# The channel transform of a Fourier mix for half of the frequencies, its even and odd parts joined by VectorE

## The chip, the cores and the metric

One core of a Trainium2 chip. The metric is the device time of one execution in microseconds (us), as a median over several executions; the profile shows one execution, whose span is some 2 us shorter than its time. TensorE is the matrix engine, VectorE and ScalarE are the element-wise engines (DVE and ACT in the profile). PE in the profile is TensorE's products and PEld the loading of their weights, one of the two operands of a product. PSUM is the memory that TensorE writes its sums into. On one core an execution counts as slow when it takes over 1.5% more than the fastest of its kernel.

## The reference, cut to what matters

A block-sparse attention (cut) gives `x`, 4 batches of 768 rows and 512 channels, fp32. Then, for each batch:

```python
X = np.fft.fft(x, axis=1)          # along the 768 rows
X = np.fft.fft(X, axis=2)          # along the 512 channels
u = x + np.real(X)
un = (u - mean(u)) / sqrt(var(u) + 1e-6)      # over the channels
out = u + np.maximum(un @ w_ch1, 0.0) @ w_ch2   # 512 -> 2048 -> 512
```

## The kernel before

All products are fp32. In a batch the row transform leaves `yt` (in the profile: `big`), whose 512 channels are folded into four groups of 128: groups 0 and 1 serve the even output channels, groups 2 and 3 the odd ones. The channel transform then works through six tiles of 128 rows. A tile takes four products with 256 columns each, and one VectorE add puts the result onto `x`:

```python
fd = bpool.tile([P, 6, HD], FP, ...)              # P = 128, HD = 256, DM = 512
fetch(out=fd, in_=dr["fd"].ap())
# ...
for half in range(2):
    # ...
    for i in range(HT):                           # HT = 3: six tiles per batch
        t = HT * half + i
        ps = bank([P, 2, HD], f"mx_{b}_{t}")
        cols = slice(P * i, P * (i + 1))
        for par in range(2):                      # even, odd output channels
            nc.tensor.matmul(ps[:, par, :], yt[:, half, 2 * par, cols], fd[:, 3 * par, :],
                             start=True, stop=False)
            nc.tensor.matmul(ps[:, par, :], yt[:, half, 2 * par + 1, cols], fd[:, 3 * par + 1 + half, :],
                             start=False, stop=True)
        xv = x[:, t, :].rearrange("p (m two) -> p two m", two=2)
        tt(xv, ps, xv, ADD)                       # one add, 512 columns
        nc.vector.bn_stats(out=bst, in_=x[:, t, :])
        nc.vector.bn_aggr(out=stat[:, i], in_=bst)
        yield
    # ... a dozen short VectorE steps: 1/sqrt(var), shift (tile `norm`)
for t in range(NST):                              # six tiles again
    # un = x * scale + shift, on ScalarE and VectorE in turn
    for d in range(NDT):
        nc.tensor.transpose(ps[:, d // 2, d % 2, :], un[:, t, P * d:P * (d + 1)], ident)   # `unt`
    # copied to u[...] by ScalarE and VectorE in turn
    yield
_right_sums(tt, lambda i: u[:, i])                # then the hidden layer `hx` may start
```

A list scheduler decides in what order the engines get this. For batches 1 to 3 it places pieces of the transform between output products of the batch before, which are the filler (`ox`, `oy`, `oz`):

```python
drive((gen_fourier(b + 1), 22, 600), (last, 12, 0))
```

In batch 0 the companion of the transform is attention work instead.

## Time and profile before

| | before |
|---|---|
| time, median of 3 (lowest to highest) | 853.1 us (852.67 to 853.25) |
| profiled span | 852.3 us |
| TensorE busy, of it | 820.0 us, 96% |
| VectorE busy | 470.9 us, 55% |
| `mx` stage of batch 2 (six tiles on TensorE) | 10.36 us |
| first `mx` product to first hidden product `hx`, batches 1, 2, 3 | 48.10, 41.52, 41.71 us |

The last row is the distance on TensorE's timeline from the first product of the changed stage to the first product of the hidden layer. It contains everything that the change touches in a batch, and it does not contain the attention at the start, whose length differs by some microseconds from one execution to the next. The lines of the page and of the timelines that carry the argument are shown in the prediction below. One more, of TensorE's timeline of before in batch 1 (columns: start us, duration us, engine, line, operation, output and inputs, shape, count, and in brackets the idle time and its releaser), shows that the stage was not wholly without waits:

```profile
277.32 1.53 PE L1045 MATMUL unt<-ident,big 128*128 128x128 f32 x12 [0.45 <-ACT big L1038]
```

### The profile page before, as it was taken

What the parts mean: (1) busy time and instruction counts of PE and PEld (TensorE: products, weight loads), DVE (VectorE), ACT (ScalarE), POOL (GpSimd) and SP (SyncE); (2) the same over time, 40 slices, a digit from 0 to 9 for tenths busy, and PEclk for the clock granted to TensorE, in tenths of its full rate; (3) what the DMA queues carried; (4) which work ended last, traced back from release to release, by engine and by line L of the source; (5) the groups of instructions that cost most, each with busy time, mean ns of one, the idle gap of its engine ahead of it and who ended that gap; (6) DMA issues with size and microseconds to landing.
All of it is one profiled execution on the core that took longest, in us unless ns stands there. A gap on an engine that the chain in (4) does not pass through costs nothing.

```text
span 852.3 us, 14372 instructions
## 1 busy us (share of the span) xinstructions
PE 820.0 (96%) x5970; PEld 573.8 (67%) x5970; DVE 470.9 (55%) x1061; ACT 230.4 (27%) x473; POOL 36.9 (4%) x44
## 2 busy tenths in 40 slices
PE   6979998999999999999999999999999999999997
PEld 5847755545557455787667875688667885686586
DVE  2487996986966343544356933443337843432352
ACT  3524666542722013122231103120321102101100
POOL 3200011003000200001000000000000000000000
PEclk8989999999999999999999999999999999999999
DMA  9998695979523273454843136403412316205001
GB/s 217 230 273 161 163 228 175 277 247 303 187 97 120 74 270 129 121 111 156 238 123 105 69 115 229 106 28 81 170 61 75 112 51 258 87 1 215 1 25 53
DMA packets 102857, 122.31 MB, mean 143 GB/s; under 512 B 50592, under 2 KB 83584, under 8 KB 102784
## 3 DMA queue, kind: packets, MB, share of 16 engines
q1 hardware_dynamic: 102240, 121.14, 48.6%
q8 instruction: 49, 0.80, 0.4%
q10 hardware_dynamic: 544, 0.17, 0.1%
q14 instruction: 24, 0.20, 0.1%
HBM read 97.18 MB, written 24.12 MB: 142 GB/s over the span
## 4 chain that ended last, share of the span: by engine, by line
PE 80%; DVE 9%; ACT 6%; DMA 2%; issue 1%; POOL 1%; ACTq 0%; DVEq 0%; POOLq 0%
PE hx L1067 18%; PE ox L1133 14%; PE hz L1067 9%; PE o L1108 7%; PE oz L1133 7%; PE hy L1067 4%; PE y L984 4%; PE oy L1133 3%; PE mx L1005 2%; PE sc L727 2%; PE mx L1007 2%; ACT kt L670 2%; ACT qt L670 2%; DVE x L552 1%; PE sc L687 1%
## 5 line engine op out<-in xcount | busy, mean ns | idle before, releaser
L1067 PE MATMUL hx<-u,w 128*128 128x384 f32 x512 | 186.1, 492 | 8.0 <-ACT h L1077 6.0
L1067 PEld LDWEIGHTS hx<-u,w 128*128 128x128 f32 x512 | 94.4, 190 | 74.7 <-ACT h L1077 9.3
L1067 PE MATMUL hz<-u,w 128*128 128x384 f32 x256 | 93.2, 486 | 0.0
L1108 PE MATMUL o<-w,h 128*128 128x512 f32 x192 | 84.7, 595 | 0.0
L1067 PEld LDWEIGHTS hz<-u,w 128*128 128x128 f32 x256 | 48.6, 190 | 33.9 <-ACT h L1084 0.2
L1133 PE MATMUL ox<-w,s 128*128 128x256 f32 x288 | 69.0, 381 | 0.4 <-DVE x L552 0.3
L1133 PE MATMUL oz<-w,s 128*128 128x256 f32 x288 | 68.6, 380 | 0.0
L1133 PE MATMUL ox<-w,h 128*128 128x256 f32 x288 | 67.3, 380 | 0.0
L1108 PEld LDWEIGHTS o<-w,h 128*128 128x128 f32 x192 | 35.8, 190 | 42.4 <-issue 40.4
L552 DVE TENSOR_TENSOR x<-ox,x 128x256 f32<-128x256 f32 x72 | 30.4, 422 | 57.5 <-PE ox L1133 57.5
L1133 PEld LDWEIGHTS oz<-w,s 128*128 128x128 f32 x288 | 54.6, 190 | 8.1 <-DVE x L552 0.8
L1133 PEld LDWEIGHTS ox<-w,s 128*128 128x128 f32 x288 | 54.1, 190 | 8.5 <-DVE x L552 1.2
L1133 PEld LDWEIGHTS ox<-w,h 128*128 128x128 f32 x288 | 54.2, 190 | 8.2
L552 DVE TENSOR_TENSOR h<-hx,h 128x384 f32<-128x384 f32 x32 | 17.8, 556 | 71.6 <-PE hx L1067 71.6
L1077 ACT COPY h<-hx 128x384 f32<-128x384 f32 x32 | 15.3, 478 | 139.4 <-PE hx L1067 127.8
L552 DVE TENSOR_TENSOR h<-hy,h 128x384 f32<-128x384 f32 x32 | 17.8, 556 | 56.9 <-PE hy L1067 53.7
L1067 PE MATMUL hy<-u,w 128*128 128x384 f32 x128 | 46.5, 486 | 0.0
L984 PE MATMUL y<-fs,fold 128*128 128x193 f32 x192 | 37.3, 337 | 0.0
L1093 ACT ACTIVATE h<-hx 128x384 f32<-128x384 f32 x32 | 15.7, 490 | 79.0 <-PE hx L1067 79.0
L984 PEld LDWEIGHTS y<-fs,fold 128*128 128x128 f32 x192 | 31.5, 191 | 8.0 <-issue 6.3
L671 DVE TENSOR_REDUCE km<-kt 128x24 f32<-128x768 f32 x16 | 15.2, 951 | 37.8 <-ACT kt L670 25.2
L1067 PEld LDWEIGHTS hy<-u,w 128*128 128x128 f32 x128 | 24.3, 190 | 17.0
(120 smaller groups left out, 1103.3 us busy)
## 6 DMA issues: line engine op xcount, KB each, us to landing
w<-dw SPq DMA_DIRECT2D x40, 896.0 KB, 5.0
words<-in_moe_w_ch_dram SPq DMA_DIRECT2D x32, 512.0 KB, 6.5
vw<-in_v_dram SPq DMA_DIRECT2D x47, 192.0 KB, 6.3
dw<-w SPq DMA_DIRECT2D x8, 896.0 KB, 7.7
kn<-in_k_dram SPq DMA_DIRECT2D x16, 384.0 KB, 4.9
qn<-in_q_dram SPq DMA_DIRECT2D x16, 384.0 KB, 5.6
vb<-in_v_dram SPq DMA_DIRECT2D x32, 192.0 KB, 5.7
out_dram<-x SPq DMA_DIRECT2D x24, 256.0 KB, 2.1
```

The source lines that it names most:

```text
L552: nc.vector.tensor_tensor(out=out, in0=in0, in1=in1, op=op)
L670: nc.scalar.copy(out=dst[D * e:D * (e + 1), s:S:2], in_=ps[D * s:D * (s + 1)])
L671: nc.vector.tensor_reduce(out=km[:, 0:nb], in_=kt[:, W:W + S].rearrange("p (n f) -> p n f", f=BLOCK), op=ALU.max, axis=AX.X)
L727: nc.tensor.matmul(ps[h][r:r + 64, i, :], kt[rows, o:o + 64], qt[rows, o:o + BLOCK], start=True, stop=True)
L984: nc.tensor.matmul(y, fgs[par][:, st, P * g:P * (g + 1)], fs[par][:, g % 2, st, :], start=(st == 0), stop=(st == HT - 1))
L1005: nc.tensor.matmul(ps[:, par, :], yt[:, half, 2 * par, cols], fd[:, 3 * par, :], start=True, stop=False)
L1007: nc.tensor.matmul(ps[:, par, :], yt[:, half, 2 * par + 1, cols], fd[:, 3 * par + 1 + half, :], start=False, stop=True)
L1067: nc.tensor.matmul(ps, w[:, a, kk, :], u[:, r, kk, :], start=start and kk == 0, stop=stop and kk == 1, skip_group_check=True)
L1077: nc.scalar.copy(out=c11, in_=X)
L1093: nc.scalar.activation(out=c21, in_=X, func=AF.Relu)
L1108: nc.tensor.matmul(ps, h[:, n, hf, P * t:P * (t + 1)], wt[2, b, j][:, 2 * hf:2 * hf + 2, :], start=(n, hf) == (0, 0), stop=(n, hf) == (NC ...
L1133: nc.tensor.matmul(ps, left[a][:, n, :], wt[2, b, j][:, r, :], start=start and n == 0, stop=stop and n == NC - 1, skip_group_check=True)
```

## The change

The real part of the transform is symmetric but for a sign: if E is the even part of output channel c and O the odd part, channel c is E + O and channel 512 - c is E - O (signs turned in the second half of the rows). So E is needed for channels 0 to 256 and O for 1 to 255 only: 512 columns per tile in place of 4 x 256 = 1024. One input row that belongs to E was stored in the group that feeds O (row 0 of group 1); it gets a product of its own with a single row, which accumulates onto E. That is the fifth product. VectorE then makes four adds of what was one, two of them reading the columns backwards. The table shrinks from 1536 to 641 columns, and the change holds for batches 1 to 3; batch 0 keeps the old form. The diff, with blank lines and the change of the returned dictionary cut:

```diff
# table
+    fd = g["fd"].reshape(P, 6, DM // 2)
+    n = DM // 4
+    odd = fd[:, 1, 1:n].copy()
+    odd[0] = 0.0
+    fm = np.concatenate([fd[:, 0, 0:n + 1], fd[:, 3, 0:n], odd, fd[:, 4, 0:n], fd[:, 1, 0:n + 1]], axis=1)
# ... fetched as `fm` where b > 0, `fd` where b == 0
+    def mix_halves(ps, y, fm, xt, half):
+        Q = DM // 4
+        e0, e1, o0, o1, row = (fm[:, a:z] for a, z in ((0, Q + 1), (Q + 1, HD + 1), (HD + 1, HD + Q),
+                                                      (HD + Q, DM), (DM, DM + Q + 1)))
+        for out, g, table, last in ((ps[:, 0:HD + 1:2], 0, e0, False), (ps[:, 1:HD:2], 2, e1, True),
+                                    (ps[:, HD + 2:DM:2], 1, o0, True), (ps[:, HD + 1:DM:2], 3, o1, True)):
+            nc.tensor.matmul(out, y[:, g], table, start=True, stop=last, skip_group_check=True)
+            if not last:
+                nc.tensor.matmul(out, y[0:1, 1], row[0:1], start=False, stop=True, skip_group_check=True)
+        low, high = xt[:, 1:HD], xt[:, HD + 1:DM]
+        tt(xt[:, 0:HD + 1], ps[:, 0:HD + 1], xt[:, 0:HD + 1], ADD)
+        tt(high, ps[:, HD - 1:0:-1], high, ADD)
+        tt(low, low, ps[:, HD + 1:DM], SUB if half else ADD)
+        tt(high, high, ps[:, DM - 1:HD:-1], ADD if half else SUB)
# in the loop over the tiles
-                ps = bank([P, 2, HD], f"mx_{b}_{t}")
+                if b:
+                    mix_halves(bank([P, DM], f"mx_{b}_{t}"), yt[:, half, :, cols], fd, x[:, t, :], half)
+                else:
+                    ps = bank([P, 2, HD], f"mx_{b}_{t}")
-                for par in range(2):
+                for par in range(0 if b else 2):
-                xv = x[:, t, :].rearrange("p (m two) -> p two m", two=2)
-                tt(xv, ps, xv, ADD)
+                if b == 0:
+                    xv = x[:, t, :].rearrange("p (m two) -> p two m", two=2)
+                    tt(xv, ps, xv, ADD)
```

More of the change, by code (lines that the diff above doesn't have):

```diff
@@ L450, in _tables @@
     fs = np.ascontiguousarray(np.moveaxis(g["fs"], 2, 0))
+    fd = g["fd"].reshape(P, 6, DM // 2)
[3 more added lines that the diff above has]
+    fm = np.concatenate([fd[:, 0, 0:n + 1], fd[:, 3, 0:n], odd, fd[:, 4, 0:n], fd[:, 1, 0:n + 1]], axis=1)
+    fm = np.ascontiguousarray(fm)
     return dict(wide=wide, near=near, sel=sel.reshape(4 * nb, 2, P), half=half.reshape(P, 2), count=count, fs=fs,
-                fd=g["fd"], ident=g["ident"])
+                fd=g["fd"], fm=fm, ident=g["ident"])
 A11, A12, S3, A22, S1, S2_, S4 = range(7)
@@ L928, in get_tables @@
             fs.append(t)
-        fd = bpool.tile([P, 6, HD], FP, tag=tag, bufs=bufs, name=f"fd_{b}")
-        fetch(out=fd, in_=dr["fd"].ap())
+        if b:
+            fd = bpool.tile([P, C["fm"].shape[1]], FP, tag=tag, bufs=bufs, name=f"fm_{b}")
+            fetch(out=fd, in_=dr["fm"].ap())
+        else:
+            fd = bpool.tile([P, 6, HD], FP, tag=tag, bufs=bufs, name=f"fd_{b}")
+            fetch(out=fd, in_=dr["fd"].ap())
         tables[b] = fs, fd
@@ L1001, in gen_fourier @@
                 t = HT * half + i
-                ps = bank([P, 2, HD], f"mx_{b}_{t}")
                 cols = slice(P * i, P * (i + 1))
-                for par in range(2):
+                if b:
+                    mix_halves(bank([P, DM], f"mx_{b}_{t}"), yt[:, half, :, cols], fd, x[:, t, :], half)
+                else:
+                    ps = bank([P, 2, HD], f"mx_{b}_{t}")
+                for par in range(0 if b else 2):
                     nc.tensor.matmul(ps[:, par, :], yt[:, half, 2 * par, cols], fd[:, 3 * par, :],
```

## The prediction

> **What bounds the kernel now.** I read the page first: engine totals, the slices, the chain of waits. Then the tile view of `mx` (the accumulator of the channel transform) and the timeline of TensorE and VectorE around one of the changed stages.
>
> ```profile
> span 852.3 us, 14372 instructions
> PE 820.0 (96%) x5970; PEld 573.8 (67%) x5970; DVE 470.9 (55%) x1061; ACT 230.4 (27%) x473; POOL 36.9 (4%) x44
> PE   6979998999999999999999999999999999999997
> PE 80%; DVE 9%; ACT 6%; DMA 2%; issue 1%; POOL 1%; ACTq 0%; DVEq 0%; POOLq 0%
> ```
>
> TensorE is the bound: 96% busy, and in slices of 21 us it drops below nine tenths only near the start and in the last slice. So removed TensorE time is worth its full length if TensorE isn't made to wait instead.
>
> ```profile
> L1005 PE MATMUL mx<-fd,big x96: 379/379/483, 75.7 to 669.3; 128*128 128x256 f32 x96
> L1007 PE MATMUL mx<-fd,big x96: 378/379/379, 78.2 to 669.7; 128*128 128x256 f32 x96
> L552 DVE TENSOR_TENSOR x<-mx,x x24: 656/682/692, 82.3 to 670.4; 128x512 f32<-128x512 f32 x24
> ```
>
> 24 tiles (6 per batch), 192 records: every fp32 product leaves two records (two passes), so a tile is 4 products of 256 columns, 8 passes. The 379 ns is a latency, not a cost; cost is the step from start to start, and the timeline has it:
>
> ```profile
> 464.00 0.59 PE L1005 MATMUL mx<-fd,big 128*128 128x256 f32 x2
> 464.43 0.59 PE L1007 MATMUL mx<-fd,big 128*128 128x256 f32 x2
> ...
> 473.93 0.59 PE L1007 MATMUL mx<-fd,big 128*128 128x256 f32 x2
> 474.36 1.89 PE L1133 MATMUL ox<-w,s 128*128 128x256 f32 x8
> ...
> 478.81 1.52 PE L1045 MATMUL unt<-ident,big 128*128 128x128 f32 x12
> 480.16 1.89 PE L1133 MATMUL ox<-w,h 128*128 128x256 f32 x8
> ```
>
> Two passes of 256 columns take 0.43 us, 0.216 each; the stage of six tiles is 474.36 - 464.00 = 10.36 us without a gap. Twelve passes of 128 columns (the transposes `unt`) take 480.16 - 478.81 = 1.35 us; without their slow start 0.109 each. Time is thus proportional to columns, and halving the columns halves it. Between the two lie output products of the previous batch (`ox`, `oz`), the filler that hides VectorE's normalisation.
>
> ```profile
> 465.93 0.69 DVE L552 TENSOR_TENSOR x<-mx,x 128x512 f32<-128x512 f32 x1 [6.05 <-PE mx L1007]
> 466.65 0.69 DVE L1012 BATCH_NORM_STATS2 bst<-x 128x6 f32<-128x512 f32 x1
> 467.38 0.18 DVE L1013 BATCH_NORM_AGGREGATE stat<-bst 128x2 f32<-128x6 f32 x1
> 468.95 1.29 DVE L552 TENSOR_TENSOR x<-mx,x 128x512 f32<-128x512 f32 x2 [1.39 <-PE mx L1007]
> ```
>
> In this stage VectorE waits for TensorE (6.05 and 1.39 us). The sums of `u` end at 487.67 + 2.69 = 490.36, and the hidden layer, which needs them, starts only at 505.52:
>
> ```profile
> 487.67 2.69 DVE L552 TENSOR_TENSOR u<-u 128x768 f32<-128x768 f32 x3
> 490.27 0.42 DVE L552 TENSOR_TENSOR x<-oz,x 128x256 f32<-128x256 f32 x1
> 490.60 0.68 DVE L552 TENSOR_TENSOR s<-s,h 128x512 f32<-128x512 f32 x1
> ```
> ```profile
> 505.52 1.45 PE L1067 MATMUL hx<-u,w 128*128 128x384 f32 x4
> ```
>
> So some 15 us of slack stand behind the stage. (490.27 to 490.60 is VectorE's step for 256 columns: 0.33 us, for a record of 0.42.)
>
> **What the Trainium skill says.** "TensorEngine Tiling (Array Packing)", Key Properties: changing the tiling mode drains TensorE. The changed kernel does that: its product with one row runs in a 32-row mode. The trace of before has such switches, at the one-column products `zq`, and agrees:
>
> ```profile
> 454.11 0.49 PE L988 MATMUL y<-fs,zq 128*1 128x193 f32 x2
> 454.53 0.59 PE L984 MATMUL y<-fs,fold 128*128 128x193 f32 x2
> 455.05 0.82 PE L988 MATMUL y<-fs,zq 128*1 128x193 f32 x4
> 455.80 3.87 PE L984 MATMUL y<-fs,fold 128*128 128x193 f32 x22
> ```
>
> An undisturbed pass of 193 columns takes 0.163 us. From 454.11 to 454.53 two passes and a switch take 0.42: the drain is 0.09. From 454.53 to 455.05 two passes and a switch take 0.52: 0.10 more. That is the weight load, which can't run ahead across the switch. "TensorE: Matmul & The Clock Gate", LDWEIGHTS, says that a load's time goes with its columns, not its rows, 128 columns at 1.2 GHz = 107 ns; it fits the 0.10, and the one-column load shows none. The one-row product loads 128 columns, so it should pay 0.10 on the way in as well; no run shows that yet.
>
> "PSUM — Partial Sum Buffer", Specifications, says that a non-contiguous access pattern slows matmuls significantly; here two products per tile write every second word. The trace of before disagrees for this form:
>
> ```profile
> 30.02 1.48 PE L660 MATMUL qk<-ident,qn 128*64 128x128 f32 x24
> ```
>
> These also write every second column, two at a time in two halves of the array: (1.48 - 0.27)/23 = 0.053 per record, 0.106 per pass in each half, full rate. I book no cost. "VectorE: DVE Perf Modes", the TRN2 errata, has (N+151)/0.96 ns for an fp32 add: 424 for 256, and the record above is 0.42. It fits.
>
> **The change part by part**, for batches 1 to 3, 18 tiles; batch 0 is untouched.
>
> TensorE, columns. Removed per tile: 8 passes x 0.216 = 1.73 us. Added: five products (129, one-row 129, 128, 127, 128 columns), 10 passes x 0.109 = 1.09 us. Saved 0.64 per tile, 3.8 per batch, 11.5 in all.
>
> TensorE, switches. By the order of instructions the one-row products of tiles 1 and 2 stand side by side, the others alone: 5 round trips per batch. Each 2 x 0.09 + 2 x 0.10 = 0.39 us; 2.0 per batch, 5.9 in all. Net on TensorE 5.6 us. The stage should take 10.36 - 3.8 + 2.0 = 8.5 us.
>
> VectorE. One add of 512 (step 0.60) becomes four of 255 to 257, 3 x 0.335 + 0.42 = 1.43 until the statistics may start: +0.75 per tile, 4.5 per batch, 13.5 in all (470.9 becomes about 484). The reads run backwards and from PSUM; I take no extra for it. Most lies in the waits of 6.05 and 1.39 us and in the slack. What reaches TensorE is where it needs a result at a fixed place in its order. Walk through batch 2, from the start of the stage: tile 0 done at 1.9; four adds and statistics to 3.9; eight adds (2.8, from 4.1, when tile 1 is there) and two statistics to 8.2; twelve adds and the norm's dozen short steps (0.08 each beside them) to 13.2; the pending `ox` add 13.6; three statistics and the first normalised tiles at 16.2 and 16.7. TensorE: stage 8.5, with output products of 0.43 around it the next use of `ox` at 14.2 (ready, 13.6), and the transposes at 16.0. It waits about 0.5 us, in batches 2 and 3, 1.0 in all. In batch 1 the order puts 12 products of 0.86 us each, 10.4 us, before the transposes, which come at 18.9 while VectorE is ready near 16: no wait.
>
> DMA. The table shrinks from 1536 to 641 columns, three times; the view shows no wait of TensorE for it. Nothing.
>
> Sum: 853.1 - 11.5 + 5.9 + 1.0 = **848.5 us**.
>
> **The rivals.** First, VectorE becomes the bound of the stage: 18 tiles give back all their 0.75 us, +13.5 against -5.6, some 861. For it: TensorE works through six tiles in 8.5 us and VectorE needs about 13, and four banks serve both. Against it: 6.05 and 1.39 us of waiting to fill, filler that the new order places later (in batch 1, 6 us more of it before the transposes), 15 us of slack. Second, the switches are free or hidden: 848.5 - 5.9 = 842.6. Against it: every such switch in the trace of before shows its 0.09. If only the load into the one-row product is hidden, 15 x 0.10 less, 847. Third, strided writes do slow the products: two of five run at half rate, 18 x 2 x 0.22 = 8 us more, 856. Against it: the transposing products above at full rate. Fourth, the whole column saving shows nowhere because another chain sets the end: 853. Against it: TensorE without a gap from the stage to the hidden layer.
>
> **Range and chances.** The mildest mix (cheaper switches, no wait) gives about 845, a VectorE that waits 1 us more per batch 851.5. Range 845.0 to 851.5. Faster by 2% would need 17 us, more than the whole column saving of 11.5: 0.01. Slower by 2% would need the first rival at full force and more: 0.01. Within 2%: 0.98.
>
> **What would show it.** TensorE's records rise by 36, VectorE's by 54. `mx` passes of 128 columns stand 0.109 apart; each one-row product has 0.2 us extra before or in it, and as much after. The stage is 8.5 us, not 6.6 (switches free) or over 10 (strided writes slow, or waiting for banks). Transposes wait for the normalised tile by about half a microsecond in batches 2 and 3. Wrong if TensorE waits for VectorE's `x` or for a bank within the stage, or if the hidden layer starts right after the sums of `u`.

## The result, and the profile after

| | before | after |
|---|---|---|
| time, median of 4 (lowest to highest) | 853.13 us (852.67 to 853.25) | 848.13 us (847.39 to 849.99) |
| ratio, 95% interval | | 0.9946 (0.9928 to 0.9963) |
| `mx` stage of batch 2, filler inside it left out | 10.36 us | 8.63 us |
| first `mx` to first `hx`, batches 1, 2, 3 | 48.10, 41.52, 41.71 | 45.59, 39.83, 40.04 |
| their sum | 131.33 | 125.46 |

A ratio, here and below, is the mean time of one kernel's fast runs over that of the other's of the same rounds, so it is not quite the ratio of the medians. The change saves 5.0 us by the medians, half a per cent: within 2%, near the 848.5 us of the prediction. The three distances account for 5.87 us, which lies inside the interval of the ratio (0.0037 x 853 = 3.2 to 0.0072 x 853 = 6.1 us).

The span and the engine totals of the page after:

```profile
span 846.1 us, 14497 instructions
PE 813.9 (96%) x6006; PEld 569.1 (67%) x6006; DVE 479.4 (57%) x1115; ACT 230.5 (27%) x473; POOL 36.3 (4%) x44
```

TensorE has 36 records more (a product of one row is two records, and there are 18) and VectorE 54 (18 tiles with 3 adds more), both as foretold. TensorE is as full as before, 96%: the saving came off the bound. The tile view of `mx` after (count, then duration in ns as lowest/median/highest, first and last start, shapes) shows what a tile now consists of:

```profile
L963 PE MATMUL mx<-fm,big x144: 273/275/377, 258.2 to 664.4; 128*128 128x128 f32 x72, 128*128 128x129 f32 x36, 128*128 128x127 f32 x36
L965 PE MATMUL mx<-fm,big x36: 270/270/373, 258.5 to 663.5; 1*128 1x129 f32 x36
```

Do not read costs out of these durations. 270 ns is how long a pass stays in the pipe, and by it the one-row product looks no dearer than the others. The cost is in the steps between starts, on TensorE's timeline of after in batch 2:

```profile
461.10 0.39 PE L963 MATMUL mx<-fm,big 128*128 128x129 f32 x2
461.41 0.48 PE L965 MATMUL mx<-fm,big 1*128 1x129 f32 x2
461.83 1.38 PE L963 MATMUL mx<-fm,big 128*128 128x128 f32 x10
463.14 0.71 PE L965 MATMUL mx<-fm,big 1*128 1x129 f32 x4
...
468.23 1.03 PE L1167 MATMUL ox<-w,s 128*128 128x256 f32 x4
...
470.59 1.03 PE L1167 MATMUL ox<-w,s 128*128 128x256 f32 x4
...
475.34 1.89 PE L1167 MATMUL ox<-w,h 128*128 128x256 f32 x8
477.54 1.52 PE L1079 MATMUL unt<-ident,big 128*128 128x128 f32 x12 [0.31 <-DVE stat L1047]
```

Read it with a pass of 128 columns at 0.11. From 461.10 to 461.41 are two passes, 0.22, and 0.09 of draining before the one-row product may start. From 461.41 to 461.83 are its own two passes, 0.22, and some 0.19 more: a load of 0.1 that isn't hidden, between its two passes, and the drain on the way out. From 461.83 to 463.14 are ten passes, 1.11, and 0.2: the load again, behind the first of them, and the drain into the next one-row product. (The single records stand 0.205 and 0.214 apart on the way in, 0.200 and 0.214 on the way out, where an undisturbed pass takes 0.111 to 0.112.) The stage ends at 470.59; with the four output passes at 468.23 taken off (0.86), it is 470.59 - 461.10 - 0.86 = 8.63 us. The eight output passes at 475.34 end at 475.34 + 8 x 0.216 = 477.07, and the transposes start at 477.54: a wait of 0.47. (The view shows 0.31 as idle, since it counts from the end of the last record.) Batch 1 has no such wait.

VectorE's timeline of after in the same stage:

```profile
462.80 0.76 DVE L560 TENSOR_TENSOR x<-mx,x 128x257 f32<-128x257 f32 x2 [5.83 <-PE mx L963]
463.47 0.74 DVE L560 TENSOR_TENSOR x<-x,mx 128x255 f32<-128x255 f32 x2
464.25 0.69 DVE L1046 BATCH_NORM_STATS2 bst<-x 128x6 f32<-128x512 f32 x1
465.20 0.43 DVE L560 TENSOR_TENSOR x<-mx,x 128x257 f32<-128x257 f32 x1 [0.26 <-PE mx L963]
...
476.88 0.52 DVE L1075 TENSOR_SCALAR big<-x,norm 128x512 f32<-128x512 f32 x1
```

Four adds from 462.80 to the statistics at 464.25 take 1.45 us (prediction: 1.43), and the wait of 1.39 us for the second tile has shrunk to 0.26. The second normalised tile ends at 476.88 + 0.52 = 477.40, just before the transposes begin. So VectorE is busy from 465.20 until the transposes, and it is now the last thing that TensorE waits for, by half a microsecond.

### The profile page after: what moved, and what is told of

Same layout as the page of the kernel before. It is cut to its first block, busy times and chain, and to the rows that moved or that the text cites. A ratio compares the mean times of both kernels' runs of the same rounds, so it can differ in the third digit from the quotient of the medians.

```text
span 846.1 us, 14497 instructions
## 1 busy us (share of the span) xinstructions
PE 813.9 (96%) x6006; PEld 569.1 (67%) x6006; DVE 479.4 (57%) x1115; ACT 230.5 (27%) x473; POOL 36.3 (4%) x44
## 4 chain that ended last, share of the span: by engine, by line
PE 79%; DVE 10%; ACT 5%; DMA 3%; issue 1%; SPq 0%; ACTq 0%; DVEq 0%
PE hx L1101 18%; PE ox L1167 13%; PE o L1142 9%; PE hz L1101 9%; PE oz L1167 7%; PE hy L1101 4%; PE y L1014 3%; PE oy L1167 3%; DVE x L560 2%; PE sc L735 2%; PE mx L963 1%; ACT qt L678 1%; ACT kt L678 1%; PE sc L695 1%; PE unt L1079 1%
```

## The experiments

The theory after the result is the prediction's own: the columns save about 11 us, ten mode switches per batch give back half, and VectorE costs about 1 us. Three rivals could give the same total by other terms: VectorE's adds cost most of what was lost; the switches are free and the strided writes cost; or part of the gain comes from the new order of work, not from the new products. Four are wrong (e2, e3, e4, e10); the others are correct. Batch 0 takes 28.8 us from its first `mx` to its first `hx` wherever its form is the old one. The measured distances, in us:

| kernel | `mx` stage, batch 2 | batch 1 | batch 2 | batch 3 | sum |
|---|---|---|---|---|---|
| before | 10.36 | 48.10 | 41.52 | 41.71 | 131.33 |
| after | 8.63 | 45.59 | 39.83 | 40.04 | 125.46 |
| e1, row product with 128 rows | 6.69 | 43.66 | 39.05 | 39.25 | 121.96 |
| e2, one add | 8.63 | 45.90 | 39.50 | 39.66 | 125.06 |
| e3, the adds alone | 10.36 | 47.32 | 41.04 | 41.35 | 129.71 |
| e4, e1 with one add | 6.70 | 44.17 | 37.62 | 37.79 | 119.58 |
| e5, four products | 6.61 | 43.57 | 39.10 | 39.41 | 122.08 |
| e6, row products in pairs | 8.38 | 45.34 | 39.58 | 39.80 | 124.72 |
| e8, e5 turned early | 6.6 | 43.81 | 35.74 | 35.96 | 115.51 |
| e10, contiguous writes | 8.63 | 45.59 | 39.85 | 40.04 | 125.48 |

### e1: the product of one row with all 128 rows

The row is padded with zeros to a full table, so that TensorE keeps its mode. Same columns, same order of instructions, same adds.

```diff
-    fm = np.concatenate([..., fd[:, 1, 0:n + 1]], axis=1)
+    row = np.zeros((P, n + 1), dtype=np.float32)
+    row[0] = fd[0, 1, 0:n + 1]
+    fm = np.concatenate([..., row], axis=1)
-                nc.tensor.matmul(out, y[0:1, 1], row[0:1], start=False, stop=True, skip_group_check=True)
+                nc.tensor.matmul(out, y[:, 1], row, start=False, stop=True, skip_group_check=True)
```

> The one-row product gets 128 rows, of which 127 of the table are zero: same columns, same result, but no change of tiling mode. Theory (columns, minus switches, minus small waits for VectorE): the mx stage falls from 8.63 to about 6.7 us per batch, the steps of 205/214 ns before and after the row product become 111. Batch 1 gains the whole 1.9 us; in batches 2 and 3 the transposes come earlier than VectorE's normalised tile and wait about 1.5 us instead of 0.3, so they gain about 0.7 each: 844.8 us. If switches alone counted: 842.3. If the switches were not what costs: 848, no change.

Measured: 843.84 us (842.79 to 844.4, 5 runs) against 853.95 for before on that chip, ratio 0.9872 (0.9845 to 0.9899). TensorE's timeline of e1 in batch 2:

```profile
458.67 0.39 PE L965 MATMUL mx<-fm,big 128*128 128x129 f32 x2
458.89 0.39 PE L967 MATMUL mx<-fm,big 128*128 128x129 f32 x2
459.12 1.28 PE L965 MATMUL mx<-fm,big 128*128 128x128 f32 x10
...
474.33 1.52 PE L1081 MATMUL unt<-ident,big 128*128 128x128 f32 x12 [1.06 <-DVE stat L1049]
```

From 458.67 to 459.12 there are now four passes in 0.45 us, where after took 0.73: the switch is gone, with 127 rows of zeros more. The stage is 6.69, so the five round trips cost 8.63 - 6.69 = 1.94 us, 0.39 each, as predicted. That is 5.8 us in three batches, but only 3.5 of them reach the sum. The last line says where the rest went: the transposes, which TensorE now reaches 1.94 us sooner, stand idle for VectorE 1.06 us. By the steps, TensorE waits 0.29 + 0.10 + 1.22 = 1.61 us in each of batches 2 and 3 (the first two for the `x` that `ox` goes into), against 0.47 in the changed kernel: 2 x 1.14 = 2.3 us, and 5.8 - 2.3 = 3.5.

### e2: one add in place of four

```diff
-        low, high = ...       # and the four adds
+        xv = xt.rearrange("p (m two) -> p two m", two=2)
+        tt(xv, ps.rearrange("p (two m) -> p two m", two=2), xv, ADD)
```

> The changed kernel's products, but VectorE adds the bank to x in one add of 512 as in the kernel before (wrong result on purpose: the even and odd parts are not joined). Theory: VectorE costs only the waits of 0.3 us at the transposes in batches 2 and 3, so 847.5, half a microsecond less than the changed kernel. Rival (VectorE sets the pace of the stage): some 4 us per batch come back, 836 to 840.

Measured: 847.53 us (846.34 to 848.68, 6 runs), ratio 0.9917 (0.9892 to 0.9941). The stage is unchanged at 8.63; the sum falls by 0.4 us: in batches 2 and 3 the distance falls by 0.33 and 0.38, and in batch 1 it rises by 0.31, since the scheduler orders this kernel's filler differently and TensorE waits there among the transposes. So VectorE's 54 adds, together with the order that they bring, cost under 1 us of time in the changed kernel. The rival that VectorE is what ate the gain falls.

### e3: the adds of the changed kernel, with the old products

```diff
-        if b:            # which table is fetched
+        if b < 0:
-        for out, g, table, last in (...):      # the five products
+        for par in range(2):
+            for k in range(2):
+                nc.tensor.matmul(ps[:, HD * par:HD * (par + 1)], y[:, 2 * par + k], fm[:, 3 * par + k * (1 + half), :],
+                                 start=k == 0, stop=k == 1)
```

> The kernel before's four products of 256 columns, but the four adds of the changed kernel (wrong result on purpose). Theory: VectorE's 4.5 us more per batch fall into its waits and into filler that the order moves; the transposes of batches 2 and 3 wait 0.5 to 0.9 us: 854.5, at most 855.5. Rival (VectorE sets the pace): 13 us more, 866.

Measured: 852.34 us (851.5 to 856.69, 7 runs), ratio 0.9971 (0.9947 to 0.9995). I had expected it a little slower than before, and it was slightly faster; the sum fell by 1.62 us. Its trace has no wait at the transposes, nor, but for 0.12 us in batch 3, the small ones that before has: 0.78, 0.48 and 0.48 us in batches 1, 2 and 3 by steps over the nominal pass, the 0.45 shown of before among them. The first transposes of e3 in batch 2:

```profile
485.00 1.47 PE L1076 MATMUL unt<-ident,big 128*128 128x128 f32 x12
```

The reason is the order: the scheduler places more output products ahead of the first transposes (9 in place of 5 in batch 1, 17 in place of 10 in batches 2 and 3), so TensorE arrives after the data. That it does so because a tile has more steps is my guess. This is a term that my prediction did not have: about 1.6 us of the result come from the order alone. It closes the account as well: from e3 to after the products change (and with them the order in batch 1, which has 12 output products there), three stages save 3 x 1.73 = 5.19, the new waits take 0.94, and 125.46 - 129.71 = -4.25. The profiled execution of e3 is its slowest, 856.69 us; its granted clock stood at 0.50 from 127 to 137 us, outside the three distances.

### e4: e1 with one add

> Both costs off: row product with 128 rows and one add of 512 (wrong result on purpose). Theory: what is left is the column saving, 18 tiles x 0.64 us = 11.5 us under the kernel before, and no wait: stage 6.7 us, 841.7 us. If the strided writes slowed the products the stage would stay above 7.5 us.

The edits are those of e1 and e2 together. Measured: 842.02 us (841.16 to 849.2, 6 runs), ratio 0.987 (0.9836 to 0.9905). The stage is 6.70, and the sum 119.58. Against e2, the same with switches, that is 5.5 us less: with VectorE's adds out of the way nearly all of the 5.8 us of switches appears in the time. Three stages save 3 x (10.36 - 6.70) = 10.98 us, the measured worth of the columns.

### e5: four products, the row without a product of its own

Group 1 feeds both O and, with its row 0, E. So one product with group 1 can serve both, if its table holds the row's columns and O's columns side by side and its output runs over the even columns of the whole bank. No mode switch, and no fifth product.

```diff
+    fm = np.concatenate([fd[:, 0, 0:n + 1], fd[:, 3, 0:n], fd[:, 4, 0:n], row, odd], axis=1)
+        e0, e1, o1, ro = (fm[:, a:z] for a, z in ((0, Q + 1), (Q + 1, HD + 1), (HD + 1, HD + Q + 1),
+                                                  (HD + Q + 1, DM + Q + 1)))
+        for out, g, table, first, last in ((ps[:, 0:HD + 1:2], 0, e0, True, False), (ps[:, 0:DM:2], 1, ro, False, True),
+                                           (ps[:, 1:HD:2], 2, e1, True, True), (ps[:, HD + 1:DM:2], 3, o1, True, True)):
+            nc.tensor.matmul(out, y[:, g], table, start=first, stop=last, skip_group_check=True)
```

> The row product shares its stationary operand with the odd product of the same group: both become one product of 256 columns with 128 rows (four products per tile, no change of tiling mode, correct result). Theory: per tile 2 x (0.110 + 0.216 + 0.109 + 0.109) = 1.09 us, stage 6.5 us against 6.7 of the full-row version; the waits for VectorE in batches 2 and 3 stay at about 1.5 us: 843.5 us, no clear difference from the full-row version. If instructions counted and not columns: stage 5.4 us.

Measured: 844.21 us (842.35 to 847.03, 6 runs) against 854.31 on that chip, ratio 0.9894 (0.9873 to 0.9915); the stage is 6.61 where I had expected 6.5. It is e1 by another way: as many columns, no switch, and much the same waits for VectorE in batches 2 and 3 (by the steps 1.76 us in each, against 1.61 in e1). A fifth product costs next to nothing beside its columns; the mode it ran in was the cost.

### e8: e5, with the first half normalised and transposed before the second half's products

If the rest of the loss in e1 and e5 is a matter of order, it should go away when VectorE finishes three tiles first, statistics, normalising and all, and TensorE transposes them while VectorE works on the other three.

```diff
+        def turn_half(ts):
+            for t in ts:
+                ...              # the normalise-and-transpose loop, unchanged
+            if b and half == 0:
+                yield from turn_half(range(HT))       # behind the norm of the first half
-        for t in range(NST):
-            ...
+        yield from turn_half(range(HT, NST) if b else range(NST))
```

> The merged form, and in batches 1 to 3 the first three tiles are normalised and transposed as soon as their half's statistics are there, ahead of the adds of the other half. Theory: the 1.5 us that TensorE waits for VectorE in batches 2 and 3 are a question of VectorE's order, not of its amount; they go, and the stage keeps 6.5 us: 840.5 us. Rival (VectorE has too much work in the stage): the wait comes back at the second three tiles or at the hidden layer, 843.5.

Measured: 840.72 us (839.43 to 842.27, 5 runs), ratio 0.9842 (0.9822 to 0.9862): the best of all, and faster than both kernels. TensorE's timeline of e8 in batch 2 (its first three tiles, then the start of the first group of transposes and the second group):

```profile
460.23 3.47 PE L965 MATMUL mx<-fm,big 128*128 128x129 f32 x24
...
474.33 0.86 PE L1040 MATMUL unt<-ident,big 128*128 128x128 f32 x6
...
488.99 1.53 PE L1040 MATMUL unt<-ident,big 128*128 128x128 f32 x12
```

Neither group of transposes has a wait behind it in brackets, nor has anything between; by the steps about 0.1 us is left at the second group. The sum of 115.51 flatters it, since in each of batches 2 and 3 eight output passes (1.73 us) moved behind the start of the hidden layer; with them it is 118.97, 3.1 us under e5, which waited 3.5 us for VectorE. VectorE runs the same 1115 instructions in both. So the wait was one of order, not of amount.

### e7 and e9: batch 0 too

e7 is e5, and e9 is e8, with the new form in batch 0 as well (`if b:` becomes true for all).

> The merged form in batch 0 as well. Theory of columns: TensorE saves another 6 x 0.64 = 3.8 us, if it is what bounds that stage: 839.7. Rival: in batch 0 VectorE, which converts weights at nine tenths busy, bounds: its 4.5 us more stand on the path and eat the gain, 843 to 848.

> Both of the last: the sum of their gains over the merged version, 836.7 if batch 0 is bound by TensorE, 840 to 845 if by VectorE.

Measured: e7 849.32 us (847.8 to 853.82, 6 runs), ratio 0.9949 (0.9924 to 0.9975); e9 847.98 us (846.48 to 848.82, 6 runs), ratio 0.9926 (0.9907 to 0.9945). Each is slower than the same kernel without it, by 5.1 and 7.3 us, although TensorE has less to do, and each lies above the range that its rival gave (843 to 848, 840 to 845): the direction was foreseen, the size was not. Batch 0 takes 36.5 and 36.2 us from `mx` to `hx`, where it took 28.8. The busy times in two stretches of batch 0 (columns: stretch and its length, busy us and records of TensorE, weight loads, VectorE, ScalarE and GpSimd, then TensorE's granted clock, DMA share and GB/s), before:

```profile
90.00:95.40 5.40, 4.27 (x119) 3.10 (x117) 5.40 (x25) 4.82 (x10) 0.00 (x0) 1.00 0.41 120
95.40:105.00 9.60, 9.04 (x203) 7.33 (x192) 9.36 (x32) 8.04 (x16) 0.00 (x0) 1.00 1.00 223
```

and in e7:

```profile
90.00:95.40 5.40, 0.43 (x2) 0.31 (x3) 5.40 (x19) 3.05 (x7) 0.00 (x0) 0.70 0.51 146
95.40:105.00 9.60, 9.58 (x160) 8.28 (x162) 7.46 (x37) 1.99 (x3) 0.00 (x0) 0.50 0.58 113
```

VectorE is busy all of the first stretch in both, 5.40 of 5.40, because the attention needs it too: in this stretch VectorE is the bound, and the adds delay what stands behind them. In e7 TensorE falls idle, as its timeline says:

```profile
95.42 1.19 PE L769 MATMUL av<-vw,p 64*32 64x65 f32 x48 [4.85 <-DVE norm L1054]
```

The releaser named there, a short step of the norm, is not the one to blame: `av` reads `p`, and VectorE's timeline has the masking multiply that makes `p` just before, behind a row of adds that began at 88.47:

```profile
94.12 0.41 DVE L562 TENSOR_TENSOR x<-x,mx 128x255 f32<-128x255 f32 x1
...
94.52 0.55 DVE L562 TENSOR_TENSOR p<-p,near 128x384 f32<-128x384 f32 x1
```

And the wait costs a second time: the clock granted to TensorE fell to 0.50 during it, at 92.1 us, and came back only at 112.6, 20.5 us later, though by its records TensorE was busy all the time from 95.42 on. So in the second stretch it was busy 9.58 of 9.60 us at half speed. In e9 the clock stood at 0.50 from 92.9 to 109.9 us. The prediction for e7 had no such term. The Trainium skill, "TensorE: Matmul & The Clock Gate", Part 1, says that an idle window of about 3.4 us takes the clock down to half. e9 agrees, where the clock fell 4.5 us after the last product before a wait of 4.76; in e7 it fell 1.6 us after the last product, sooner than a whole idle window. That VectorE is nearly full in this stretch was to be read in the profile of before, and it is a good reason to leave batch 0 alone. Whether another order, with the multiply ahead of the adds, would save batch 0 is not tested.

### e6: row products in pairs

The order of the five products is turned round in every second tile, so that one-row products of neighbouring tiles stand side by side: four round trips in place of five.

```diff
+        one = (ps[:, 0:HD + 1:2], y[0:1, 1], row[0:1])
+        prods = [one] + prods if t % 2 else prods + [one]
```

> The one-row product kept, but last in even tiles and first in odd tiles, so that two of them stand side by side twice per batch: 4 round trips of tiling mode instead of 5 by the order of instructions (correct result). Theory: the cost goes by the trip, 0.39 us each, so the stage falls from 8.63 to 8.25 us per batch and the kernel by at most 1.2 us, less what the transposes of batches 2 and 3 wait for VectorE: 847.5. If the cost went by one-row products (6 in either kernel), the stage stays 8.63.

Measured: 846.83 us (846.04 to 847.17, 4 runs) against 853.45 on that chip, ratio 0.9917 (0.9901 to 0.9934). The stage is 8.38, where one trip less should have made it 8.63 - 0.39 = 8.24. Each of the four trips left has the steps of after (0.205 and 0.214 in, 0.200 and 0.214 out), and the missing 0.14 us is a single hold-up at the start of the stage. I take it for a wait for the copy of `y`, which the turned order needs in another sequence; that is argued, not shown.

### e10: contiguous writes

The same products write their columns side by side in PSUM, so that the results land in the wrong channels.

```diff
-        for out, g, table, last in ((ps[:, 0:HD + 1:2], 0, e0, False), (ps[:, 1:HD:2], 2, e1, True),
-                                    (ps[:, HD + 2:DM:2], 1, o0, True), (ps[:, HD + 1:DM:2], 3, o1, True)):
+        for out, g, table, last in ((ps[:, 0:Q + 1], 0, e0, False), (ps[:, Q + 1:HD + 1], 2, e1, True),
+                                    (ps[:, HD + 1:HD + Q], 1, o0, True), (ps[:, HD + Q:DM], 3, o1, True)):
```

> The changed kernel's five products written to neighbouring columns of the bank instead of every second one (wrong result on purpose). Theory: strided writes are free: passes stay 0.111 us apart, stage 8.63 us, same time as the changed kernel, 848. If the 2 ns between 0.111 and the 0.109 of the transposes come from the stride: stage 8.5 us.

Measured: 849.39 us (848.56 to 852.97, 4 runs), ratio 0.996 (0.9934 to 0.9987); the stage is 8.63, and the steps are those of after. Writing every second word costs nothing here. Nor is it the reason why these passes stand 0.111 apart instead of 0.109.

## Why the prediction was right

The prediction said 848.5 us, and 848.13 was measured. By its own steps, for three batches:

| term | predicted | measured | by |
|---|---|---|---|
| columns | -11.5 | -10.98 | stage of e4 against before, x 3 |
| mode switches | +5.9 | +5.8 | stage of after against e1, x 3 |
| waits for VectorE | +1.0 | +0.94 | 0.47 at the transposes, batches 2 and 3 |
| order of the filler | not in it | -1.62 | e3 against before |
| sum | -4.6 | -5.86 | the traces of before and after: -5.87 |

- **Columns.** Right. The size is 0.5 us off, because these passes stand 0.111 to 0.112 us apart and not 0.109 as the transposes do. Why is open; the stride is ruled out by e10 and the single-row mode by e1, which has the same steps.
- **Switches.** Right, in the amount per trip (0.387 against 0.39), in their number (five per batch) and in where they show: a drain each way and the weight load that can't run ahead, also for the product of one row. e1 takes them out and finds them. (That the mode is one of 32 rows, as the prediction says, no view shows; e1 shows that the cost goes when the product has 128 rows.) The second rival (switches free) falls with it, and e4 against e2 shows their worth in the time.
- **VectorE.** Right about what reaches TensorE: nothing in batch 1, half a microsecond in batches 2 and 3, and transposes at 477.54 - 461.10 = 16.44 us after the start of the stage, against 16.0 + 0.5. The busy time was mis-sized: +8.5 us (470.9 to 479.4) against +13.5. The adds themselves came near it: from e2 with one add (467.6) to after is 11.8 us. But e2 lies 3.3 us under before with the same number of VectorE instructions (1061), and e5 4.5 us under e8 with 1115 in each, so the busy time moves by some microseconds with the order of work alone, which the prediction did not count. The first rival (VectorE the bound of these stages) is refuted by e2 and e3.
- **Strided writes.** Right to book nothing: the third rival falls with e10. The working misread the change here: it has two of the five products write every second word, but in the diff all five do, so a rival at half rate would have cost 18 x 5 x 0.22, some 20 us, and not 8. The fourth (another chain sets the end) falls with every kernel that took TensorE time away and got faster.
- **The term that was missing.** The prediction took TensorE to be "without a gap from the stage to the hidden layer" before the change. It had small waits there in each of the three batches, 1.7 us together, and the new order of the filler removed nearly all of them. A view of waits on the transposes of before would have shown the largest. With 1.6 against a gain of 5 it didn't move the class, and the columns' 0.5 stood against it. That the median came within 0.4 us of the number is luck in part: the three distances gained 5.87 us where the prediction had 4.6, and the medians show 5.0; the difference between these two lies outside the distances or in the spread of the runs.

The whole-run figures can't separate terms of 1 us: the medians of before, taken anew beside each set of runs, lie between 853.1 and 854.3, and single runs of one kernel spread by 0.6 to 8 us. The terms above rest on distances inside one trace each, which repeat within some hundredths where nothing was changed (e10 against after: 0.02 in the sum).

## What to carry to other kernels

On a full TensorE, halving the columns of these products paid nearly in proportion (10.98 us of the 11.5 that the columns promised), but keep every product in the same tiling mode: padding one row with zeros to 128, or letting it ride along in another product with the same stationary operand, saved 0.39 us per trip, the worth of three and a half passes. Work moved to another engine was nearly free here only where that engine had slack (batches 1 to 3, not batch 0), and then its order decides: let it finish first what TensorE needs first. The kernel to keep is e8, with four products, the first half turned early, and batch 0 left as it was: 840.72 us against 854.31.

## What the Trainium skill lacked or had wrong

- "PSUM — Partial Sum Buffer", Specifications (TRN2): it says that any non-contiguous access pattern slows matmuls significantly. For fp32 products of 127 to 129 columns that write every second word, it doesn't: the stage took 8.63 us with and without the stride.
- "TensorEngine Tiling (Array Packing)", Key Properties: it says that a change of mode drains TensorE, without a number. Here a product with one row among products with 128 cost 0.387 us per round trip: about 0.09 of drain and 0.1 of exposed weight load, each way.
- "TensorE: Matmul & The Clock Gate", Back-to-back issue gap: its formula for the full clock, N/2.4 + 2.5 ns, doesn't say how an fp32 product enters into it. Here such a product is two records (a transpose is one), and each stands apart as the formula has it for twice the columns: 0.163 us for 193 and 0.216 for 256 columns. The `mx` passes of 128 columns stand 0.111 to 0.112 apart, where this gives 0.109.
